# Inverse softmax sums of the first batch by PE transposes, all transposed exponentials copied by ScalarE, and a planner with transfer classes and a clock model

## Chip, core and metric

One core of one Trainium2 chip runs one program. The metric is the device time of one execution in microseconds (us). A kernel's time is the median of its runs.

## What is computed

Attention over 4 batches with 12 heads (448 positions, head size 64), then two feed-forward stages over the 1792 tokens. Everything is float32; the kernel reaches the precision with pairs of fp32r values (high part and rest) and three matmuls for each product.

```python
def _attn_ref(q, k, v, g_q, g_k):
    q_n, k_n = (rmsnorm(q, g_q), rmsnorm(k, g_k))
    scores = scale * np.matmul(q_n, k_n.transpose(0, 1, 3, 2))
    scores = scores - np.max(scores, axis=-1, keepdims=True)
    attn = np.exp(scores)
    attn = attn / (np.sum(attn, axis=-1, keepdims=True) + 1e-09)
    return np.matmul(attn, v)

def _moe_ref(x, w_in, w_out):
    h = x @ w_in
    g = h * np.cos(h)
    return g @ w_out

def _moe2_ref(x, w_in, w_out, a, b):
    h = x @ w_in
    P = a[0] + a[1] * h + a[2] * h2 + a[3] * h3
    Q = 1.0 + np.abs(b[0]) * np.abs(h) + np.abs(b[1]) * h2
    return (P / (Q + 1e-6)) @ w_out
```

## The kernel before, in words

**Stages.** Heads are taken in pairs, six to a batch, so there are 24 pairs `(b, j)`. The six pairs of batch 0 run first. Then, for each batch `b`, the first feed-forward stage (`moe1_first`, `moe1_second`) runs, and between its matmuls stand the pairs of batch `b + 1`. After batch 3 the second stage (`moe2`) runs.

**One pair.** `att_load` loads q and k, `att_norm` normalizes them, `att_t` transposes them on TensorE. `att_s` makes the scores in four chunks; for each chunk VectorE takes the negated row maximum (`mx<-t`) and ScalarE the exponential, whose row sums go to a column of the tile `sums` (`e<-t,mx`). `att_vt` transposes the exponentials on TensorE into PSUM tiles `t` of a ring, and a copy brings them to SBUF as `et`; this copy is a task that either ScalarE or VectorE may take ("AV"). `att_va` multiplies `et` with v into the one PSUM tile `x_ps`, over four blocks `kb`. The last block is followed by a VectorE product with the inverse sums, `rb<-x_ps,rb`. Since `x_ps` has one buffer, the first `x_ps` matmul of the next pair waits for this product.

**Inverse sums.** In `x_ps` the tokens lie along the free dimension, but `sums` has them along partitions. So the function `inverse` (in `att_s`) makes the reciprocals on VectorE and transposes them in 32 x 32 blocks (`rows<-sums`), four transfers write them to DRAM (`rd<-rows`), and two transfers read them back, each row spread over 64 partitions (`rb<-rd`).

**Weights.** Each 768 KB unit of weights `(m, f)` arrives as raw words (`raw<-in_moe_w_in`, `raw<-in_moe_w_out`; `m` 0 and 1 are the first stage's two matrices). `decode` takes it apart: three VectorE steps, a ScalarE copy of the high part, a GpSimd subtraction for the rest. Decoded units are stored to DRAM (`wd`). The first seven are used straight from SBUF (`w`, stored by `wd<-w`); eight more, the list `early`, are decoded into the raw tile, stored by `wd<-raw`, and loaded again by `w<-wd` when one of the seven weight tiles comes free. The first matmuls `h_ps<-g,w` of batch 0 need the units (1,0) to (1,3); (1,0) is one of the seven, (1,1) to (1,3) are `early` ones.

**What sets the order.** The Python code runs through the TensorE order, which is fixed by the code. All work of the other engines is handed to `Clock.do` as tasks with a planned duration and dependencies. `Clock` keeps a model time and emits a task on its engine's in-order queue (V, A, G, or S for the DMA queue of SyncE) when the model says that the engine would take it; `rank` picks among ready tasks. The function `body` rehearses the whole kernel `REHEARSALS` times, derives due times from each rehearsal (`plan`), and builds the program with the due times of the rehearsal with the lowest model time. A task with `size` is a transfer: the model adds `size / RATE` to the time at which the DMA engines are free. So numbers in these calls move instructions, though they are no part of the computation.

All instructions show one line, 277, that of the helper which records them.

Of the kernel before, what the change touches and what calls it, by code (L numbers as in the profile page):

```python
# [11 lines left out]
F32 = mybir.dt.float32  # L12
F32R = mybir.dt.float32r
I32 = mybir.dt.int32
AF = mybir.ActivationFunctionType
# [5 lines left out]
P, NC = 128, 4  # L21
# [7 lines left out]
EPS = 1e-6  # L29
REHEARSALS = 12  # L30
EXP, SIN = "natural_log_exp_and_others", "trig_and_small"
# [9 lines left out]
class Clock:  # L41

    WAIT, LOAD, RATE, QUEUE, LAND, AHEAD = 4.0, 1.28, 0.362, 4.0, 1.25, 1.0
    FROM_PE, TO_PE, LAT = 0.19, 0.11, 0.035
    OVER = {"V": 0.085, "A": 0.1, "G": 0.0, "S": 0.0}

    def __init__(self, due=None):
        self.t, self.n, self.named = 0.0, 0, {}  # L50
        self.free = dict.fromkeys(("V", "A", "G", "S"), 0.0)
        self.todo = {e: [] for e in self.free}
        self.tab, self.dma = None, 0.0
        self.port = {"V": 0.0, "G": 0.0}
        self.slots = deque([0.0] * 8, 8)
        self.due, self.all, self.count = due, [], {}

    def do(
# [44 lines left out]
    def rank(self, k, e, start):  # L103
        other = k.tab is not None and k.tab != self.tab and start - k.ready < self.WAIT
        second = len(k.eng) > 1 and e != next(iter(k.eng))
        if k.due is None:
            return other, k.prio + 2 * second, k.ready, k.n
        return other, k.due + 1.0 * second, k.ready, k.n

# [27 lines left out]
    def step(self, until=math.inf):  # L137
# [25 lines left out]
        if k.size:  # L163
            self.dma = max(self.dma, start + self.LAND) + k.size / self.RATE
            end = max(end, self.dma) + 0.9
            for _ in range(k.parts):
                self.slots.remove(math.inf)
            self.slots.extend([end] * k.parts)
        k.end = end
        k.eng = {eng: k.eng[eng]}  # L170
# [31 lines left out]
    def pe(self, dur):  # L202
        self.t += dur
        while self.step(self.t - self.AHEAD):
            pass

    def plan(self, last):

        due = {}
        for k in reversed(self.all):  # L210
            k.lst = k.need - self.TO_PE
            for x in k.succ:
                k.lst = min(k.lst, x.lst - self.LAT)
            k.lst -= next(iter(k.eng.values())) + (k.size / self.RATE + 2.0 if k.size else 0)
            old = last.get(k.name, math.inf) if last else math.inf
            due[k.name] = k.lst if math.inf in (k.lst, old) else 0.3 * k.lst + 0.7 * old
        return due
# [86 lines left out]
class Kernel:  # L304
# [87 lines left out]
    def decode(self, m, f, keep=True, p=1):  # L392
# [36 lines left out]
        def store():  # L429
# [5 lines left out]
        k = self.raw_load = ck.do(  # L435
            "S", 0.48, load, last, p=p, size=0.786, behind=self.raw_load, name=who + ("load",)
        )
        for i, d in enumerate((0.55, 0.95, 0.95)):
# [11 lines left out]
        k2 = ck.do(  # L450
            "S", 0.39, store, k, p=p, size=0.786, key=("wd", m, f), name=who + ("store",)
        )
# [6 lines left out]
    def load_w(self, m, f):  # L459
# [6 lines left out]

        return t, self.ck.do("S", 0.36, load, ("wd", m, f), p=1, size=0.786)

# [25 lines left out]
    def att_load(self, b, j):  # L494
# [3 lines left out]
        for i, n in ((1, "k"), (0, "q")):  # L498
# [29 lines left out]
            k = ck.do("G", 0.3 if i else 0.35, blank, p=0)  # L528
            s["load"][i] = [k, ck.do("S", 1.95 if i else 2.3, load, p=0 if b == 0 else 1, size=0.23, parts=4 - i)]
        return s  # L530
# [4 lines left out]
    def att_load_v(self, s):  # L535
# [11 lines left out]

        s["vk"] = self.ck.do("S", 1.7, load, p=1, size=0.23, parts=3)

# [107 lines left out]
    def att_s(self, s, c):  # L657
# [43 lines left out]
        def inverse():  # L701
# [4 lines left out]
            nc.vector.reciprocal(t, t)  # L706
            nc.vector.transpose(u, sm)

# [11 lines left out]

        rd = self.rd[s["b"] * NJ + s["j"]]
        k = ck.do("V", 0.66, inverse, *s["ek"], p=1, port=True)
        k = ck.do("S", 1.3, write, k, p=0, size=0.004, parts=4)
        s["smk"][:] = [k]
# [11 lines left out]
    def att_vt(self, s, kb):  # L736
# [26 lines left out]
        n = 2 * S if kb < NM else NC * P  # L763
        et = s["et", kb] = p.tile([P, 2 * S], F32, tag="et", name="et", bufs=2)[:, :n]
        if kb < NM:
            k1 = ck.do("AV", (0.6, 0.69), lambda e: self.copy(e, et[:, : NC * P], tp[0]), p=0)
            k2 = ck.do(
                "AV", (0.5, 0.55), lambda e: self.copy(e, et[:, NC * P :], tp[1][:, : NM * P]), p=0
            )
            tu[0][1].append(k1)  # L770
            tu[1][1].append(k2)
            s["etk", kb] = [k1, k2]
        else:
            k1 = ck.do("AV", (0.6, 0.69), lambda e: self.copy(e, et, tp[0]), p=0)
            tu[0][1].append(k1)
            s["etk", kb] = [k1]

    def att_va(self, s, kb):
# [3 lines left out]
        if kb == 0:  # L782
            ck.need(s["vk"])
            s["xp"] = self.x_ring.tile(ck)
            spread, k = s["rbk"]
            s["rbk"] = ck.do("S", 1.25, spread, k, self.rb_used, p=0, size=0.23, parts=2)
        (xp, users), et, v = s["xp"], s.pop(("et", kb)), s["v"]
# [9 lines left out]
        if kb == NM:  # L797
# [21 lines left out]
            kept.append(k)  # L819
            self.rb_used = k  # L820

    def att_v(self, s, kb):
# [103 lines left out]
    def moe1_second(self, b, d, fs, gs, y):  # L926
# [26 lines left out]
        if fs[-1] == NF - 1:  # L953
# [8 lines left out]

            kept.append(ck.do("S", 0.36, store, k, key=("xd", b, d), size=0.46))

    def load_x(self, b, js=range(NJ), p=1):
        ck = self.ck
        for j in js:
# [7 lines left out]
            self.x[b, j] = x  # L975
            kept.append(ck.do("S", 0.45, load, ("xd", b, j), p=p, key=("x", b, j), size=0.46))

    def moe2(self, tiles, G, after_x):
# [9 lines left out]
        def second(t, fs, gs, wo):  # L988
# [27 lines left out]
            if fs[-1] == NF - 1:  # L1016
                kept.append(ck.do("S", 0.45, lambda: store(o, t), k, size=0.4))

# [346 lines left out]
```

## Time and profile before

| | us |
|---|---|
| median of 3 runs | 1287.27 (1286.4 to 1288.6) |
| the profiled execution | 1285.99 |
| its span, first to last instruction | 1283.8 |
| TensorE busy | 1231.9 (96%) |
| VectorE, ScalarE, GpSimd busy | 899.8, 668.8, 286.9 |
| mean granted TensorE clock | 0.99 of full |

The span is shorter than the execution by 2.2 us, which lie around it. "Busy" is the time in which at least one instruction of the engine ran. TensorE (PE in the rows) is busy almost throughout, so what can be won is its idle time, the stretches at a lower granted clock (PEclk below 1.00), and matmuls that are left out. An idle stretch is put down to the event that ended it. DVE is VectorE, ACT ScalarE, POOL GpSimd, SPq the queue of SyncE, which issues nearly all transfers.

### The profile page before, as it was taken

The numbers are of one execution on the slowest core, as the hardware profiler recorded it, in microseconds if no ns is written. First come the engines' busy times: TensorE is split into PE (matmuls) and PEld (weight loads), VectorE is DVE, ScalarE is ACT, GpSimd is POOL, SyncE is SP. The second block draws the span as 40 slices with busy tenths as digits, with TensorE's granted clock in tenths as the row PEclk, the third lists the DMA queues.
The fourth block names the chain that finished last, engine by engine and source line by source line (L and its number), as shares of the span: only waits on it lengthen the run. The fifth ranks groups of instructions, "written<-read, shape, count | busy, mean of one in ns | idle before, by whom it ended". The sixth has DMA issues, their size and how long they took to land.

```text
span 1283.8 us, 18219 instructions
## 1 busy us (share of the span) xinstructions
PE 1231.9 (96%) x6576; PEld 1051.6 (82%) x6576; DVE 899.8 (70%) x1443; ACT 668.8 (52%) x1277; POOL 286.9 (22%) x363
## 2 busy tenths in 40 slices
PE   6798899899999999999999999999999999999998
PEld 4456667678877778877778999999999999999998
DVE  7787889985778766878766443775767576567663
ACT  6564557653665544755544223675544455554540
POOL 4555355551425231325122110100000000000000
PEclk9899799999999999999999999999999999999999
DMA  4666987877897689888689997624141825132312
GB/s 122 188 189 237 314 313 222 284 259 279 281 330 255 221 305 339 283 288 292 226 311 370 379 372 289 259 74 148 50 148 50 311 109 208 50 148 78 122 48 86
DMA packets 133562, 283.62 MB, mean 221 GB/s; under 512 B 57953, under 2 KB 91745, under 8 KB 133473
## 3 DMA queue, kind: packets, MB, share of 16 engines
q1 hardware_dynamic: 133280, 282.46, 62.7%
q8 instruction: 52, 0.85, 0.3%
q14 instruction: 38, 0.30, 0.1%
q0 software_dynamic: 192, 0.00, 0.0%
HBM read 215.49 MB, written 66.93 MB: 220 GB/s over the span
## 4 chain that ended last, share of the span: by engine, by line
PE 72%; DMA 12%; DVE 6%; ACT 3%; SPq 3%; POOL 2%; issue 2%; POOLq 0%; DVEq 0%; ACTq 0%
PE h_ps L277 43%; PE o_ps L277 18%; PE t L277 8%; DMA rb<-rd 4%; PE x_ps L277 3%; SPq L277 3%; DMA qk<-in_k 2%; DVE w L277 2%; DMA raw<-in_moe_w_out 2%; DMA raw<-in_moe_w_in 2%; DMA w<-wd 2%; DVE k L277 1%; DMA wd<-raw 1%; ACT k L277 1%; POOL w L277 1%
## 5 line engine op out<-in xcount | busy, mean ns | idle before, releaser
L277 PE MATMUL h_ps<-x,w 128*128 128x448 f32 x2250 | 486.4, 369 | 5.0 <-DVE k L277 3.1
L277 PEld LDWEIGHTS h_ps<-x,w 128*128 128x128 f32 x2250 | 418.1, 188 | 50.2 <-issue 10.5
L277 PE MATMUL h_ps<-g,w 128*128 128x448 f32 x1152 | 251.1, 372 | 14.7 <-DMA w<-wd 9.8
L277 PEld LDWEIGHTS h_ps<-g,w 128*128 128x128 f32 x1152 | 214.9, 189 | 42.8 <-issue 9.1
L277 PE MATMUL o_ps<-w,g 128*128 128x384 f32 x1344 | 244.6, 337 | 0.0
L277 PEld LDWEIGHTS o_ps<-w,g 128*128 128x128 f32 x1344 | 237.1, 188 | 1.9
L277 DVE SCALAR_TENSOR_TENSOR w<-raw,w 128x768 int32<-128x768 int32 x128 | 136.1, 1066 | 0.9
L277 ACT ACTIVATE e<-t,mx 128x448 f32<-128x448 f32 x168 | 104.8, 633 | 35.0 <-DVE mx L277 34.8
L277 POOL TENSOR_TENSOR raw<-w,raw 128x768 fp32r<-128x768 f32 x40 | 74.8, 1870 | 195.3 <-ACT raw L277 188.4
L277 PE MATMUL x_ps<-et,v 128*64 128x448 f32 (+1 forms) x384 | 91.6, 568 | 7.5 <-issue 5.9
L277 DVE TENSOR_REDUCE mx<-t 128x1 f32<-128x448 f32 x168 | 95.1, 616 | 5.1 <-PE t L277 4.9
L277 PEld LDWEIGHTS t<-ident,e 128*128 128x128 f32 (+1 forms) x696 | 76.3, 138 | 26.3 <-issue 21.5
L277 PE MATMUL t<-kt,qt 64*128 64x448 f32 (+1 forms) x504 | 85.5, 408 | 9.2 <-DVE kt L277 4.0
L277 PE MATMUL t<-ident,e 128*128 128x128 f32 (+1 forms) x696 | 89.1, 277 | 1.2 <-ACT e L277 1.2
L277 PEld LDWEIGHTS t<-kt,qt 64*128 64x128 f32 (+1 forms) x504 | 51.6, 194 | 41.3 <-issue 18.6
L277 ACT ACTIVATE g<-q 128x448 fp32r<-128x448 f32 x64 | 36.9, 577 | 88.3 <-DVE q L277 88.2
L277 ACT ACTIVATE k<-h_ps,cc 128x448 int32<-128x448 f32 x61 | 38.3, 630 | 64.7 <-PE h_ps L277 64.7
L277 ACT ACTIVATE q<-h_ps,na 128x448 f32<-128x448 f32 x64 | 46.3, 724 | 39.1 <-PE h_ps L277 38.5
L277 ACT ACTIVATE r<-v,cc 128x448 f32<-128x448 f32 x64 | 42.8, 668 | 45.4 <-DVE v L277 44.3
L277 DVE TENSOR_TENSOR q<-q,h_ps 128x448 f32<-128x448 f32 x64 | 39.7, 620 | 37.7 <-ACT w L277 36.5
L277 DVE SCALAR_TENSOR_TENSOR v<-v,r 128x448 f32<-128x448 f32 x64 | 40.0, 625 | 37.1 <-ACT r L277 35.2
L277 DVE TENSOR_TENSOR y<-h_ps,y 128x448 f32<-128x448 f32 x72 | 44.4, 618 | 25.2 <-PE h_ps L277 24.8
(80 smaller groups left out, 1371.4 us busy)
## 6 DMA issues: line engine op xcount, KB each, us to landing
w<-wd SPq DMA_DIRECT2D x168, 768.0 KB
wd<-raw SPq DMA_DIRECT2D x40, 768.0 KB
raw<-in_moe_w_in SPq DMA_DIRECT2D x32, 768.0 KB
raw<-in_moe_w_out SPq DMA_DIRECT2D x32, 768.0 KB
wd<-w SPq DMA_DIRECT2D x24, 768.0 KB
xd<-x SPq DMA_DIRECT2D x24, 448.0 KB
x<-xd SPq DMA_DIRECT2D x24, 448.0 KB
rb<-rd SPq DMA_DIRECT2D x48, 112.0 KB
```

The source lines that it names most:

```text
L277: inst = fn(*args, **kw)
```

## The change

1. **Inverse sums in batch 0.** `inverse` leaves out its block transpose, and no `rd` and `rb` transfers are made. A new function `att_rows`, called before the last `x_ps` block, makes eight PE transposes of a column of `sums` that is broadcast to 128 columns, into two PSUM tiles, and ScalarE copies two 64 x 448 pieces to `rb`. Batches 1 to 3 keep the way through DRAM.
2. **Copies of `et`.** All go to ScalarE.
3. **Planner.** 40 rehearsals in place of 12. A transfer's `size` is now its own time in us, negative for writes, with latencies READ 2.2 and WRITE 1.5 and a delay LATE 1.0 until it counts as done. TensorE's model time passes more slowly after idle stretches. A change of ScalarE's table no longer ranks behind everything; it adds 2.0 to the due time.

The diff, cut to its core:

```diff
-REHEARSALS = 12
+REHEARSALS = 40
...
     def rank(self, k, e, start):
-        other = k.tab is not None and k.tab != self.tab and start - k.ready < self.WAIT
+        other = k.tab is not None and k.tab != self.tab
...
-        return other, k.due + 1.0 * second, k.ready, k.n
+        return k.due + 1.0 * second + 2.0 * other, k.ready, k.n
...
         if k.size:
-            self.dma = max(self.dma, start + self.LAND) + k.size / self.RATE
-            end = max(end, self.dma) + 0.9
+            lag = self.READ if k.size > 0 else self.WRITE
+            self.dma = max(self.dma, end - k.eng["S"] / k.parts + lag) + abs(k.size)
+            end = max(end, self.dma)
...
-            "S", 0.48, load, last, p=p, size=0.786, behind=self.raw_load, name=who + ("load",)
+            "S", 0.48, load, last, p=p, size=2.9 if m % 2 == 0 else 2.5, behind=self.raw_load, name=who + ("load",)
...
-            "S", 0.39, store, k, p=p, size=0.786, key=("wd", m, f), name=who + ("store",)
+            "S", 0.39, store, k, p=p, size=-1.9, key=("wd", m, f), name=who + ("store",)
...
-        return t, self.ck.do("S", 0.36, load, ("wd", m, f), p=1, size=0.786)
+        return t, self.ck.do("S", 0.36, load, ("wd", m, f), p=1, size=2.0)
...
-            nc.vector.transpose(u, sm)
+            if s["b"]:
+                nc.vector.transpose(u, sm)
...
-        k = ck.do("V", 0.66, inverse, *s["ek"], p=1, port=True)
-        k = ck.do("S", 1.3, write, k, p=0, size=0.004, parts=4)
+        k = ck.do("V", 0.66 if s["b"] else 0.45, inverse, *s["ek"], p=1, port=True)
+        if s["b"] == 0:
+            s["rbk"] = None, k
+            return
+        k = ck.do("S", 1.3, write, k, p=0, size=-0.3, parts=4)
...
-            k1 = ck.do("AV", (0.6, 0.69), lambda e: self.copy(e, et[:, : NC * P], tp[0]), p=0)
...
+        for t, to, x, dur in parts:
+            eng, dur = "A", dur[0]
+            k = ck.do(eng, dur, lambda e="A", to=to, x=x: self.copy(e, to, x), p=0)
...
+        if kb == NM and s["b"] == 0:
+            self.att_rows(s)
...
+    def att_rows(self, s):
+
+        nc, ck = self.nc, self.ck
+        ck.need(s["rbk"][1])
+        tiles = [self.at_tile() for _ in range(2)]
+        for h, (tp, _) in enumerate(tiles):
+            for k in range(h * NM, h * NM + NC):
+                a = (k - h * NM) * P
+                nc.tensor.transpose(
+                    tp[:, a : a + P], s["sm"][:, k : k + 1].to_broadcast([P, P]), self.ident[:]
+                )
+        ck.pe(0.77)
+
+        def rows():
+            rb = s["rb"] = self.at_p.tile([P, S], F32, tag="rb", name="rb", bufs=1)
+            for h, ((tp, _), r) in enumerate(zip(tiles, HALVES)):
+                nc.scalar.activation(rb[r], tp[r, h * SL : h * SL + S], AF.Copy)
+
+        s["rbk"] = ck.do("A", 1.0, rows, self.rb_used, p=0)
```

What it moves is seen at two places. On TensorE, pair 0 of batch 0, before (`x_ps<-et,v` are the blocks of the product with v, `t<-kt,qt` the scores of the next pair, `t<-ident,e` the transposed exponentials):

```order
L277 MATMUL x_ps<-et,v 64x448 x2
L277 MATMUL t<-kt,qt 128x448 x6
L277 MATMUL x_ps<-et,v 64x448 x2
L277 MATMUL t<-kt,qt 128x448 x6
L277 MATMUL t<-ident,e 128x128 x7
```

And now:

```order
L293 MATMUL x_ps<-et,v 64x448 x2
L293 MATMUL t<-kt,qt 128x448 x6
L293 MATMUL t<-ident,sums_63 128x128 x8
L293 MATMUL x_ps<-et,v 64x448 x2
L293 MATMUL t<-kt,qt 128x448 x6
L293 MATMUL t<-ident,e 128x128 x7
```

The eight transposes are the only difference; six such blocks stand in the program, one for each pair of batch 0, and the rest of TensorE's order is as it was.

On SyncE's queue, from the end of batch 0's attention on, before (stores of decoded units, `wd<-raw`, and loads of them, `w<-wd`):

```order
L277 DMA rb<-rd 64x448 x2
L277 DMA raw<-in_moe_w_out 128x1536
L277 DMA wd<-w 128x1536
L277 DMA raw<-in_moe_w_out 128x1536
L277 DMA wd<-w 128x1536
L277 DMA wd<-raw 128x1536 x2
L277 DMA w<-wd 128x1536
L277 DMA raw<-in_moe_w_in 128x6x256
L277 DMA wd<-raw 128x1536
L277 DMA w<-wd 128x1536
L277 DMA raw<-in_moe_w_in 128x6x256
L277 DMA w<-wd 128x1536
```

And now:

```order
L293 DMA raw<-in_moe_w_out 128x1536
L293 DMA wd<-w 128x1536
L293 DMA wd<-raw 128x1536
L293 DMA raw<-in_moe_w_in 128x6x256
L293 DMA wd<-raw 128x1536 x2
L293 DMA raw<-in_moe_w_in 128x6x256 x2
L293 DMA wd<-raw 128x1536
L293 DMA w<-wd 128x1536 x2
L293 DMA raw<-in_moe_w_out 128x1536
L293 DMA wd<-raw 128x1536
L293 DMA w<-wd 128x1536 x2
```

Four stores of `early` units now stand before the first load of one, in place of two, and the first two loads follow each other directly. On GpSimd's queue the steps of these four units stand ahead of the small transfer `ab<-in_moe_a`, which in the order before stood ahead of all of them. In the whole program 85 copies `et<-t` leave VectorE for ScalarE; the number of table loads on ScalarE is 21 in both.

## Rows read from the trace of the kernel before

**Rows 1.** The page: span, TensorE's share, and the group of transposes of exponentials.
```profile
span 1283.8 us, 18219 instructions
...
PE 1231.9 (96%) x6576; PEld 1051.6 (82%) x6576; DVE 899.8 (70%) x1443; ACT 668.8 (52%) x1277; POOL 286.9 (22%) x363
...
L277 PE MATMUL t<-ident,e 128*128 128x128 f32 (+1 forms) x696 | 89.1, 277 | 1.2 <-ACT e L277 1.2
```

**Rows 2.** Busy us of each engine by stretch, granted clock, DMA share, GB/s.
```profile
0.00:102.00 102.00, 81.63 (x462) 48.92 (x462) 78.53 (x153) 62.24 (x156) 55.63 (x103) 0.95 0.60 169
56.00:62.00 6.00, 6.00 (x27) 3.65 (x27) 3.79 (x8) 2.31 (x5) 3.90 (x6) 0.69 0.52 176
78.00:88.00 10.00, 8.95 (x41) 4.98 (x42) 8.68 (x16) 6.21 (x17) 7.20 (x9) 0.83 0.64 205
102.00:142.00 40.00, 28.75 (x131) 24.15 (x130) 33.33 (x45) 20.61 (x33) 15.45 (x11) 0.83 0.74 269
132.00:137.00 5.00, 2.30 (x6) 1.33 (x5) 4.97 (x6) 1.99 (x3) 1.81 (x1) 0.50 1.06 375
137.00:142.00 5.00, 5.00 (x20) 3.84 (x20) 4.96 (x8) 3.17 (x5) 2.16 (x2) 0.53 0.63 221
240.00:255.00 15.00, 10.78 (x58) 8.04 (x58) 15.00 (x21) 9.99 (x22) 7.96 (x11) 1.00 0.86 282
```

**Rows 3.** Waits of PE over the whole span: us, times, longest.
```profile
PE h_ps L277 <- DMA w<-wd: 11.7, 5, 5.0
PE t L277 <- DVE qk L277: 9.6, 2, 9.2
PE x_ps L277 <- issue: 5.9, 1, 5.9
```

**Rows 4.** Timeline, 38 to 64 us: start, duration, instruction, idle time before it.
```profile
38.88 1.09 PE L277 MATMUL t<-ident,qk 128*128 128x128 f32 x8
...
39.81 0.93 PE L277 MATMUL t<-ident,e 128*128 128x128 f32 x7
...
55.09 0.62 DVE L277 TENSOR_TENSOR rb<-x_ps,rb 128x448 f32<-128x448 f32 x1 [4.86 <-DMA rb<-rd]
...
55.82 1.76 PE L277 MATMUL x_ps<-et,v 128*64 128x448 f32 x4 [5.87 <-issue]
...
57.51 1.97 PE L277 MATMUL t<-ident,qk 128*128 128x128 f32 x8
```

**Rows 5.** Timeline, 96 to 142 us: the first loads of early units and what they wait for.
```profile
110.67 1.38 PE L277 MATMUL h_ps<-x,w 128*128 128x448 f32 x6
...
112.62 0.20 ACT L277 ACTIVATE bb<-ab 128x2 f32<-128x2 f32 x1 [7.36 <-DMA ab<-in_moe_b]
...
115.53 4.29 SPq L277 DMA_DIRECT2D wd<-raw  x2
...
119.92 0.37 SPq L277 DMA_DIRECT2D w<-wd  x1
...
125.80 0.85 PE L277 MATMUL h_ps<-g,w 128*128 128x448 f32 x3 [2.04 <-DMA w<-wd]
...
131.69 1.46 PE L277 MATMUL h_ps<-g,w 128*128 128x448 f32 x3 [5.04 <-DMA w<-wd]
...
135.85 1.46 PE L277 MATMUL h_ps<-g,w 128*128 128x448 f32 x3 [2.70 <-DMA w<-wd]
```

**Rows 6.** Groups of copies of `et`, 0 to 102 us: busy us, mean ns of one.
```profile
L277 DVE COPY et<-t 128x512 f32<-128x512 f32 x12 | 8.2, 681 | 0.0
L277 DVE COPY et<-t 128x384 f32<-128x384 f32 x10 | 5.5, 550 | 1.2 <-issue 1.1
L277 ACT ACTIVATE et<-t 128x512 f32<-128x512 f32 x12 | 7.1, 594 | 2.4 <-issue 1.9 <-PE t L277 0.5
L277 ACT ACTIVATE et<-t 128x384 f32<-128x384 f32 x8 | 3.9, 491 | 0.1
```

**Rows 7.** Waits of VectorE over the whole span, the product with the inverse sums.
```profile
DVE rb L277 <- DMA rb<-rd: 33.0, 15, 5.5
```

More of the change, by code (lines that the diff above doesn't have):

```diff
@@ L41 @@
 class Clock:
[L45 removed]
+    WAIT, LOAD, QUEUE, AHEAD, LATE = 4.0, 1.28, 4.0, 1.0, 1.0
+    READ, WRITE, WINDOW = 2.2, 1.5, 3.413
     FROM_PE, TO_PE, LAT = 0.19, 0.11, 0.035
@@ L56, in __init__ @@
         self.due, self.all, self.count = due, [], {}
+        self.window, self.half = [0, 0.0], True
     def do(
@@ L103, in rank @@
     def rank(self, k, e, start):
-        other = k.tab is not None and k.tab != self.tab and start - k.ready < self.WAIT
+        other = k.tab is not None and k.tab != self.tab
         second = len(k.eng) > 1 and e != next(iter(k.eng))
         if k.due is None:
-            return other, k.prio + 2 * second, k.ready, k.n
-        return other, k.due + 1.0 * second, k.ready, k.n
+            return other and start - k.ready < self.WAIT, k.prio + 2 * second, k.ready, k.n
+        return k.due + 1.0 * second + 2.0 * other, k.ready, k.n
     def candidate(self, e):
@@ L168, in step @@
             self.slots.extend([end] * k.parts)
+            end += self.LATE
         k.end = end
@@ L202, in pe @@
     def pe(self, dur):
-        self.t += dur
+        while dur > 1e-9:
+            n = int(self.t // self.WINDOW)
+            if n > self.window[0]:
+                idle, part = n > self.window[0] + 1, self.window[1] / self.WINDOW
+                self.half = idle or part < (0.62 if self.half else 0.5)
+                self.window = [n, 0.0]
+            rate = 0.53 if self.half else 1.0
+            d = min(dur / rate, (n + 1) * self.WINDOW - self.t + 1e-6)
+            self.window[1] += d
+            self.t += d
+            dur -= d * rate
         while self.step(self.t - self.AHEAD):
@@ L213, in plan @@
                 k.lst = min(k.lst, x.lst - self.LAT)
-            k.lst -= next(iter(k.eng.values())) + (k.size / self.RATE + 2.0 if k.size else 0)
+            k.lst -= next(iter(k.eng.values())) + (abs(k.size) + self.READ + self.LATE if k.size else 0)
             old = last.get(k.name, math.inf) if last else math.inf
@@ L528, in att_load @@
             k = ck.do("G", 0.3 if i else 0.35, blank, p=0)
-            s["load"][i] = [k, ck.do("S", 1.95 if i else 2.3, load, p=0 if b == 0 else 1, size=0.23, parts=4 - i)]
+            s["load"][i] = [k, ck.do("S", 1.95 if i else 2.3, load, p=0 if b == 0 else 1, size=1.3 if i == 0 else 0.9, parts=4 - i)]
         return s
@@ L546, in load @@
                 nc.sync.dma_start(out=v[r, 2 * NM], in_=src[h, SM:])
-        s["vk"] = self.ck.do("S", 1.7, load, p=1, size=0.23, parts=3)
+        s["vk"] = self.ck.do("S", 1.7, load, p=1, size=1.1, parts=3)
     def att_norm(self, s):
@@ L764, in att_vt @@
         et = s["et", kb] = p.tile([P, 2 * S], F32, tag="et", name="et", bufs=2)[:, :n]
+        parts = [(tu[0], et[:, : NC * P], tp[0], (0.6, 0.69))]
         if kb < NM:
-            k1 = ck.do("AV", (0.6, 0.69), lambda e: self.copy(e, et[:, : NC * P], tp[0]), p=0)
[L767 to L776, printed above, removed]
+            parts.append((tu[1], et[:, NC * P :], tp[1][:, : NM * P], (0.5, 0.55)))
+        s["etk", kb] = []
+        for t, to, x, dur in parts:
+            eng, dur = "A", dur[0]
+            k = ck.do(eng, dur, lambda e="A", to=to, x=x: self.copy(e, to, x), p=0)
+            t[1].append(k)
+            s["etk", kb].append(k)
     def att_va(self, s, kb):
@@ L785, in att_va @@
             spread, k = s["rbk"]
-            s["rbk"] = ck.do("S", 1.25, spread, k, self.rb_used, p=0, size=0.23, parts=2)
+            if spread:
+                s["rbk"] = ck.do("S", 1.25, spread, k, self.rb_used, p=0, size=0.7, parts=2)
+        if kb == NM and s["b"] == 0:
+            self.att_rows(s)
         (xp, users), et, v = s["xp"], s.pop(("et", kb)), s["v"]
@@ L820, in att_va @@
             self.rb_used = k
+    def att_rows(self, s):
[14 more added lines that the diff above has]
+        s["rbk"] = ck.do("A", 1.0, rows, self.rb_used, p=0)
+        for _, users in tiles:
+            users.append(s["rbk"])
     def att_v(self, s, kb):
@@ L961, in store @@
                 )
-            kept.append(ck.do("S", 0.36, store, k, key=("xd", b, d), size=0.46))
+            kept.append(ck.do("S", 0.36, store, k, key=("xd", b, d), size=-1.1))
     def load_x(self, b, js=range(NJ), p=1):
@@ L975, in load_x @@
             self.x[b, j] = x
-            kept.append(ck.do("S", 0.45, load, ("xd", b, j), p=p, key=("x", b, j), size=0.46))
+            kept.append(ck.do("S", 0.45, load, ("xd", b, j), p=p, key=("x", b, j), size=1.15))
     def moe2(self, tiles, G, after_x):
@@ L1016, in second @@
             if fs[-1] == NF - 1:
-                kept.append(ck.do("S", 0.45, lambda: store(o, t), k, size=0.4))
+                kept.append(ck.do("S", 0.45, lambda: store(o, t), k, size=-0.95))
         def before(fs, gs, order):
```

## The prediction

> **What bounds the kernel now.** I read the page first. TensorE is busy for 1231.9 of 1283.8 us [rows 1], so the work on TensorE sets the end and the other engines count where TensorE waits for them or runs at half clock. The second view, the waits of TensorE, shows how little there is to win [rows 3]: 9.6 us for normalized q and k, nearly all of it the first load, which this change leaves alone; 11.7 us in five pieces for weights loaded back (`w<-wd`); and 5.9 us before a single `x_ps` matmul. The third view, busy time by stretch [rows 2], says where it lies: TensorE is idle for 20.4 of the first 102 us (102.00 - 81.63), the attention of batch 0, and for 11.3 of the next 40 (40.00 - 28.75), the first matmuls of the feed-forward stage. What follows can give back a few us only. The fourth view, the timeline, says what holds each of the two large waits.
>
> The wait of 5.87 us before `x_ps` has no releaser named. VectorE's product with `rb` ended 0.1 us before it (55.09 + 0.62 against 55.82), and had itself stood idle for 4.86 us for the transfer `rb<-rd` [rows 4]. So the way of the sums through DRAM was late, the one `x_ps` buffer stayed taken, and TensorE stood still. After it the clock is down: 0.69 granted in 56 to 62 us [rows 2], and eight transposes are spread over more time (1.97 us) than before it (1.09) [rows 4]. Since the clock has two levels, 2.4 and 1.2 GHz, 0.69 over 6 us means 3.7 us at the lower one ((1 - 0.69) x 2 x 6).
>
> The second large wait is three pieces of 2.04, 5.04 and 2.70 us, each ended by a `w<-wd` load [rows 5]. The first of these loads was issued at 119.92, right behind two stores of decoded units that held SyncE's queue for 4.29 us; and the matmul it feeds started at 125.80, 5.9 us after the issue. The stores were late since the decode was late: ScalarE stood 7.36 us for the small transfer `ab` and could only then go on with the decoded units [rows 5].
>
> **The change, part by part.** The sum is made against the profiled execution, 1286.0 us (span 1283.8 and 2.2 around it); the median shown is 1.3 us above it.
>
> *A, batch 0's sums.* Gone: the stall, 5.87 us, and the half-rate work behind it, 1.9 us (half of 3.7, TensorE being busy for all of 56 to 62). No other pair stalled this way [rows 3]. Gone too are 36 transfers from SyncE's queue and six block transposes from VectorE; they are worth nothing by themselves, because neither queue nor engine holds TensorE elsewhere in this stage. Added: 48 transposes on TensorE. The nearest row are eight transposes whose successor starts 0.93 us later (38.88 to 39.81) [rows 4], so six blocks take 5.6 us. That they cost nothing is excluded, since TensorE takes them in order and is the bound; at half clock a block took up to 1.97 us, so the other end is 11.8 us. I take 5.6, because most of this stage runs at full clock (0.95 over 0 to 102) [rows 2].
>
> Here a rule of the Trainium skill speaks against the change. "TensorE: Matmul & The Clock Gate", Part 4, PE-mode transpose, gives about 275 ns for a transpose and says that the full clock does not engage for them; by it 48 would be 13.2 us (an estimate from that page). The trace agrees on the duration of one, 277 ns mean [rows 1], but not on what a row of them costs, since they overlap.
>
> The two ScalarE copies to `rb` for each pair lie between a 384- and a 512-element copy, 0.49 to 0.59 us each [rows 6]; they run beside the last `x_ps` block and the 26 matmuls of other pairs that follow before `x_ps` is wanted again. Nothing on the path. Their cover is gone if ScalarE's queue is late; that is a rival below. The new wait on TensorE, for the reciprocals, is short work on VectorE of sums that were complete before the first block of the pair; everything on TensorE would queue behind it.
>
> In 78 to 88 us TensorE is idle for 1.05 us and at half clock for 3.4 us ((1 - 0.83) x 2 x 10) [rows 2], behind exponentials and a copy that were late. VectorE is busy 8.68 of these 10 us and loses copies, while ScalarE gains them. Idle time and half-rate work together are 1.05 + 1.7 = 2.75 us; I take half, 1.4. A is 5.87 + 1.9 + 1.4 - 5.6 = 3.6 us.
>
> *B, early weights.* Now four stores stand before the first load of an early unit instead of two, and their decode stands before `ab` on GpSimd. VectorE has room for it: it gives up 13.7 us of copies in the first 102 us (8.2 + 5.5) [rows 6]. The first two loads can then be issued when weight tiles come free, after the six matmuls that end at 112.05, while the matmul that waited first was due at 123.8 (125.80 - 2.04) [rows 5]: 11.7 us, and a load took 5.9. The third stands behind one more store, of a unit decoded after `ab`; it is what is late next, and I leave 2.5 us for it. So of 9.8 us of waiting (2.04 + 5.04 + 2.70) 7.3 go. The clock was at 0.50 and 0.53 in 132 to 142, where TensorE was busy for 2.30 and 5.00 us [rows 2]; all of the first and 94% of the second were at the lower level, and half of that, 3.5 us, goes with the wait. B is 10.8 us. Its ends are nothing, if the wait only moves to another unit, and 13.3.
>
> *C, later batches.* 63 more copies leave VectorE. In 240 to 255 us VectorE is busy for all 15.00 us, while TensorE is busy for 10.78 [rows 2]: 4.2 us lost to VectorE. I take half, 2.1. All other tasks of batches 1 to 3 are reordered too; these stretches lose little now, and I take nothing, with 4 us either way for the range. Table loads stay at 21.
>
> Sum: 3.6 + 10.8 + 2.1 = 16.5 us. 1286.0 - 16.5 = 1269.5, and with 1.3 for the median 1270.8; I say 1271.
>
> **The rivals.** *ScalarE becomes the bound in batch 0.* It was busy for 62.2 of 102 us [rows 2]. Now it takes 22 copies (12 x 0.594 + 10 x 0.491 = 12.0 us), and twelve `rb` copies (5.9 to 7.1), so some 81 us, with steps of four decodes on top, in a stage that is to shrink to 98. For: exponentials, q, k and the copies now queue on one engine. Against: its copies follow each other closely, and the copies on it are shorter than on VectorE (594 against 681 ns). If it binds, A turns into a loss of some 3 us: 1271 + 3.6 + 3 = 1278. The Trainium skill, "TensorEngine Tiling (Array Packing)", PSUM Bottleneck, advises using both engines for emptying PSUM, which is this rival. No row here yet shows ScalarE full.
>
> *The early loads stay late*, since reordered stores or raw loads hold SyncE's queue for them: B is lost but for 2 us, 1271 + 8.8 = 1280.
>
> *Transposes that don't overlap.* A row of eight that does not overlap takes 2.2 us (8 x 277 ns [rows 1]) in place of 0.93; six rows are 7.7 us more, 1279. The overlap in the rows speaks against it.
>
> *Slower: the sums' transfers of batches 1 to 3.* 18 pairs still fetch `rb` through DRAM, and the new order may put it behind more 768 KB loads. VectorE already waits 33.0 us for `rb` in 15 cases, of which only one stopped TensorE [rows 3, 7]. Each that does would cost what the one did, 5.87 + 1.9 = 7.8 us. Two would cost most of the gain; from the third on it is slower: 1271 + 23.4 = 1294. Against it: the matmuls between give most of these pairs cover now.
>
> *The planner's order changes nothing on the chip* where it was meant to: only the stall goes and the transposes come, 5.87 + 1.9 - 5.6 = 2.2 us, 1285 in the median.
>
> **How the numbers follow.** The forecast, 1260 to 1276, has 0.62: its low end takes all that B and C could give and 4 us more (1271 - 2.5 - 2.1 - 4 = 1262, rounded out), its high end 4 us less and a part of the transposes' upper end. ScalarE 0.1, late loads 0.1, transposes 0.04, no effect 0.05, slower 0.09. The range 1260 to 1281 holds the forecast and the three rivals that end by 1280; it leaves out the last two (0.14), and little below. A difference under 0.2% (2.6 us) can't be told from no change. Faster takes the forecast and the first three rivals, 0.86; same 0.05; slower 0.09.
>
> **What would show it.** Right: no `x_ps` wait of several us in the first 100 us and a clock at full in 50 to 62; the last `x_ps` of batch 0 some 4 us earlier; no more than one wait for `w<-wd` before 140 us, of under 3 us. Six rows of eight transposes with a successor after 0.93 us. VectorE's busy time lower by 50 us or more, ScalarE's higher by about as much. Wrong: TensorE waiting for `et` or `e` of ScalarE for more than 5 us in batch 0; early loads issued later than the stage's first matmuls; or a `rb<-rd` that ends an `x_ps` wait in a later batch.

## Result and the profile after

| us | before | after |
|---|---|---|
| median of 4 runs, measured together | 1287.43 (1286.40 to 1288.60) | 1276.57 (1273.58 to 1278.12) |
| profiled execution | 1285.99 | 1273.58 |

The ratio is 0.9913 [0.9893, 0.9933]: 10.9 us faster, where 16.5 were forecast. The profiled execution is the fastest of its four, so its gain of 12.4 us is a little above the median's.

The page after, with the same group as in [rows 1]:

```profile
span 1271.8 us, 18275 instructions
...
PE 1232.2 (97%) x6624; PEld 1055.3 (83%) x6624; DVE 860.4 (68%) x1360; ACT 710.0 (56%) x1373; POOL 273.6 (22%) x356
...
L293 PE MATMUL t<-ident,e 128*128 128x128 f32 (+1 forms) x696 | 88.6, 277 | 0.0
```

VectorE is busy 39 us less (50 were expected) and ScalarE 41 us more: the copies have moved. TensorE's busy time stays, with 48 transposes more. The stretches of [rows 2], after:

```profile
0.00:102.00 102.00, 83.97 (x491) 52.81 (x492) 79.12 (x136) 78.14 (x190) 59.77 (x100) 0.98 0.65 192
...
56.00:62.00 6.00, 6.00 (x41) 3.69 (x39) 5.66 (x9) 5.59 (x13) 3.19 (x5) 1.00 0.84 289
78.00:88.00 10.00, 9.85 (x64) 5.71 (x63) 8.16 (x15) 7.24 (x18) 3.99 (x10) 1.00 0.56 193
102.00:142.00 40.00, 34.45 (x174) 28.26 (x173) 29.65 (x43) 23.58 (x43) 17.47 (x22) 0.96 0.88 317
234.00:249.00 15.00, 10.82 (x58) 8.03 (x57) 14.45 (x23) 10.24 (x20) 8.66 (x10) 1.00 0.78 254
```

The clock in 56 to 62 is 1.00 (0.69 before), and TensorE works 5.7 us more in 102 to 142. The last row is 6 us earlier than its counterpart, since the same work stands 6 to 7 us earlier there; TensorE's share of it hasn't changed (10.78 before). ScalarE is busy 78 of the first 102 us, near the 81 of the prediction. The waits of TensorE, as [rows 3]:

```profile
PE t L293 <- DVE qk L293: 9.6, 2, 9.3
PE h_ps L293 <- DVE k L293: 9.5, 7, 3.2
PE t L293 <- ACT e L293: 4.3, 4, 2.6
PE h_ps L293 <- DVE qt L293: 3.8, 1, 3.8
PE t L293 <- POOL qk L293: 2.6, 2, 2.3
PE h_ps L293 <- DMA w<-wd: 2.2, 4, 0.8
```

The `x_ps` stall is gone and loads hold TensorE for 2.2 us instead of 11.7. `h_ps` now waits 9.5 us for VectorE's `k` (5.7 before, in pieces of at most 1.6 us); new are its wait for `qt` and one for `qk` of GpSimd. Where the time went shows when the same matmuls of the same order start in both profiled executions (the last column is before minus after, from unrounded times):

| matmul | before | after | after is ahead by |
|---|---|---|---|
| first transposes of q, k of pair 1 | 16.8 | 19.1 | -2.3 |
| `x_ps` behind the second block of sums | 45.6 | 49.4 | -3.9 |
| transposes of e after the old stall | 59.3 | 56.1 | 3.2 |
| `x_ps` behind the third block | 64.7 | 62.4 | 2.3 |
| `x_ps` after the first `h_ps` | 72.3 | 76.0 | -3.6 |
| batch 0's last `x_ps` (end) | 102.1 | 105.4 | -3.3 |
| transposes of q, k in the first `h_ps` stretch | 122.1 | 128.7 | -6.6 |
| scores behind the early loads | 137.2 | 132.1 | 5.1 |
| first transposed e of batch 1 | 160.4 | 156.8 | 3.6 |
| last `x_ps` of batch 3 (end) | 668.2 | 657.3 | 10.9 |

Three losses stand in this table beside the gains. The timeline of TensorE after shows them, and one block of transposes (start, duration, instruction, idle time before it):

```profile
19.10 1.12 PE L293 MATMUL t<-ident,qk 128*128 128x128 f32 x4 [2.27 <-POOL qk L293]
...
35.13 1.09 PE L293 MATMUL t<-ident,sums 128*128 128x128 f32 x8
36.15 0.97 PE L293 MATMUL x_ps<-et,v 64*64 64x448 f32 x4
...
73.03 1.49 PE L293 MATMUL h_ps<-x,w 128*128 128x448 f32 x3 [3.81 <-DVE qt L293]
74.32 1.70 PE L293 MATMUL t<-ident,e 128*128 128x128 f32 x7
...
123.42 4.86 PE L293 MATMUL h_ps<-x,w 128*128 128x448 f32 x15 [3.24 <-DVE k L293]
```

**At 17 us** TensorE waits for normalized q and k of pair 1. In the new order pair 1's second sum of squares stands behind two scaled copies on VectorE and runs at 13.71 instead of 11.99, and GpSimd's chain for q and k begins at 14.90 instead of 13.34. The first decode of a weight unit stands among VectorE's next steps; it begins at 14.66 and so can't have delayed the start of that chain. Within the chain another 0.7 us are lost.

**At 69 us** the first `h_ps` of the feed-forward stage waits 3.81 us for `qt`, which is no operand of it. Up to here the tiles of `t` come from a ring of seven, five `at_ps` and two `early_ps`; then the two `early_ps` places become `h_ps`. Counted in the program, 71 tiles are taken before this point, and after the change 77, two more for each of three pairs. So the ring stands elsewhere, and the two places now are those of pair 5's transposed q and k (the last pair of batch 0, counted from 0), which were only just made. The matmul can't write before ScalarE and VectorE have read them, and ScalarE comes to them late (timeline of ScalarE after):

```profile
69.78 0.58 ACT L293 ACTIVATE x<-rb 128x448 fp32r<-128x448 f32 x1
70.25 0.85 ACT L293 ACTIVATE w<-w 128x768 fp32r<-128x768 f32 x1
70.98 0.63 ACT L293 ACTIVATE sq<-qk 128x512 f32<-128x512 f32 x1
71.50 0.69 ACT L293 ACTIVATE qt<-t,gg 128x512 fp32r<-128x512 f32 x1
...
118.36 0.20 ACT L293 ACTIVATE bb<-ab 128x2 f32<-128x2 f32 x1 [7.89 <-DMA ab<-in_moe_b]
118.59 0.64 ACT L293 ACTIVATE k<-h_ps,cc 128x448 int32<-128x448 f32 x1
```

**At 120 us** the last two of these rows show why `h_ps` waits for `k`: in ScalarE's queue, ahead of `k<-h_ps`, stands a step on the coefficients `ab`, and that tiny transfer is late. VectorE's queue is held by the same coefficients (`na<-ab`, the first row below, from VectorE's timeline). The issue stands on GpSimd's queue behind decode steps, more of them than before:

```profile
116.08 0.17 DVE L293 TENSOR_SCALAR na<-ab 128x4 f32<-128x4 f32 x1 [3.28 <-DMA ab<-in_moe_a]
...
110.55 1.84 POOL L293 TENSOR_TENSOR raw<-w,raw 128x768 fp32r<-128x768 f32 x1 [2.30 <-ACT raw L293]
112.33 0.62 POOL L293 DMA_DIRECT2D ab<-in_moe_a  x1
112.95 0.54 POOL L293 DMA_DIRECT2D ab<-in_moe_b  x1
```

The gain of this stretch is in the loads: the first two are issued at 114.74 (119.92 before), behind the stores and 14.8 us ahead of the first `h_ps<-g,w` at 129.51:

```profile
114.74 0.93 SPq L293 DMA_DIRECT2D w<-wd  x2
```

### The profile page after: what moved, and what is told of

Same layout as the page of the kernel before. It is cut to its first block, busy times and chain, and to the rows that moved or that the text cites. A ratio compares the mean times of both kernels' runs of the same rounds, so it can differ in the third digit from the quotient of the medians.

```text
span 1271.8 us, 18275 instructions
## 1 busy us (share of the span) xinstructions
PE 1232.2 (97%) x6624; PEld 1055.3 (83%) x6624; DVE 860.4 (68%) x1360; ACT 710.0 (56%) x1373; POOL 273.6 (22%) x356
## 4 chain that ended last, share of the span: by engine, by line
PE 80%; DMA 4%; DVE 2%; ACT 1%; issue 1%; POOL 1%; SPq 0%; DVEq 0%; POOLq 0%; ACTq 0%
PE h_ps L293 48%; PE o_ps L293 18%; PE t L293 9%; PE x_ps L293 4%; DMA w<-wd 3%; DMA raw<-in_moe_w_in 1%; DVE w L293 1%; DVE k L293 0%; DMA rb<-rd 0%; ACT k L293 0%; POOL w L293 0%; ACT w L293 0%; DVE x L293 0%; ACT L293 0%; SPq L293 0%
## 5 line engine op out<-in xcount | busy, mean ns | idle before, releaser
L293 PE MATMUL h_ps<-g,w 128*128 128x448 f32 x1152 | 248.2, 369 | 8.1 <-DVE k L293 6.2
L293 DVE SCALAR_TENSOR_TENSOR w<-raw,w 128x768 int32<-128x768 int32 x128 | 139.7, 1095 | 1.1
L293 ACT ACTIVATE et<-t 128x512 f32<-128x512 f32 (+1 forms) x168 | 82.2, 554 | 25.4 <-PE t L293 25.1
L293 DVE SCALAR_TENSOR_TENSOR k<-k,h_ps 128x448 f32<-128x448 int32 x61 | 37.7, 619 | 57.2 <-ACT k L293 56.9
L293 ACT ACTIVATE r<-v,cc 128x448 f32<-128x448 f32 x64 | 42.8, 669 | 48.7 <-DVE v L293 47.6
L293 ACT ACTIVATE raw<-w 128x768 fp32r<-128x768 f32 x40 | 33.8, 847 | 58.0 <-DVE w L293 50.8
```

Of the source, the lines that this page charges most:

```text
L293: inst = fn(*args, **kw)
```

## The experiments

Every run is compared with the kernel before, measured beside it: 1285.58 us beside e1 to e4, 1284.83 beside e5 to e8 and 1286.80 beside e9 to e12. Between these groups the ratios say more than the microseconds. "Batch 0" is the end of its last `x_ps`, "stage" the time from there to batch 1's first transposed e, "batches 1 to 3" from there to the last `x_ps`, each in the profiled execution alone. The same kernel differs there by up to 2 us (the change and e5), and e1's profiled execution is the slowest of its ten, 3.8 us above the median.

| run | us | ratio [95%] | batch 0 | stage | batches 1 to 3 |
|---|---|---|---|---|---|
| before | | 1 | 102.1 | 58.3 | 507.8 |
| the change, first measured | 1276.57 | 0.9913 [0.9893, 0.9933] | 105.4 | 51.4 | 500.5 |
| e1 rows only | 1285.97 | 1.0010 [0.9998, 1.0022] | 101.8 | 50.8 | 512.1 |
| e2 copies only | 1290.89 | 1.0057 [1.0037, 1.0077] | 105.1 | 51.1 | 512.9 |
| e3 planner only | 1283.12 | 0.9978 [0.9963, 0.9993] | 100.4 | 62.8 | 501.4 |
| e10 rows and copies | 1298.08 | 1.0093 [1.0069, 1.0117] | 113.4 | 56.8 | 503.4 |
| e11 all but copies | 1279.15 | 0.9943 [0.9921, 0.9965] | 102.3 | 52.9 | 504.5 |
| e12 all but rows | 1281.66 | 0.9963 [0.9951, 0.9974] | 104.1 | 60.6 | 502.2 |
| e5 the whole change again | 1276.49 | 0.9930 [0.9905, 0.9955] | 105.2 | 52.4 | 502.5 |
| e4 and ring turned | 1283.27 | 0.9980 [0.9967, 0.9994] | 99.7 | 59.9 | 505.3 |
| e6 and `ab` early | 1271.01 | 0.9885 [0.9848, 0.9922] | 104.4 | 47.6 | 502.6 |
| e7 ring and `ab` | 1273.48 | 0.9905 [0.9874, 0.9935] | 99.8 | 52.0 | 505.4 |
| e8 ring, `ab`, start | 1274.68 | 0.9914 [0.9883, 0.9944] | 102.3 | 49.8 | 505.5 |
| e9 transposes twice | 1277.07 | 0.9930 [0.9906, 0.9954] | 108.2 | 50.0 | 503.9 |

### One part alone

**e1**, the kernel before with the sums of batch 0 by transposes:

```diff
...
+        if s["b"] == 0:
+            s["rbk"] = None, k
+            return
...
+        if kb == NM and s["b"] == 0:
+            self.att_rows(s)
...
```

> The kernel before with the inverse sums of batch 0 by PE transposes, and nothing else of the change. Theory A (the sums give little by themselves: a stall of 5.9 us and 1.9 us of half-rate work go, 48 transposes cost 5.6 us, and six more PSUM tiles shift the ring so that the first h_ps matmul of batch 0 waits for q and k copies): 1284 to 1289 us, no x_ps wait of several us before 100 us, and a new wait of h_ps of 1 to 4 us between 65 and 80 us. Rival (the sums are what the change gains by): 1279 us or less.

The stall is gone and batch 0 is 0.3 us shorter, not 3.6: a wait of `h_ps` for `kt`, 3.59 us at 69.46, has come in, the ring's shift again, under the old planner. The early loads went forward too (three stores stand ahead of the first load instead of two; 0.5 us of `w<-wd` waits before 160), a thing this edit doesn't touch: with other tasks the planner makes another order everywhere. At 258 us the kernel was 11.7 us ahead; it lost this in batches 1 to 3 and behind them, 4.6 of it in one wait for `k` at 677.

**e2**, the kernel before with all copies of `et` on ScalarE:

```diff
...
-            k1 = ck.do("AV", (0.6, 0.69), lambda e: self.copy(e, et, tp[0]), p=0)
+            k1 = ck.do("A", 0.6, lambda e="A": self.copy(e, et, tp[0]), p=0)
```

> The kernel before with all copies of et on ScalarE, and nothing else of the change. Theory D (VectorE, freed of the copies, decodes early units sooner, so their stores come before the first load): waits for w<-wd before 145 us fall from 9.8 to under 4 us, the time is 1277 to 1283, while the x_ps wait for rb stays. Rival M (the new transfer model in the planner puts the stores ahead): waits for w<-wd stay at 7 us or more and the time is within 3 us of 1287.

The waits for early loads go here as well, yet the kernel is slower: `x_ps` waits 3.2 us at 57 and 1.9 at 87, and `t` 5.4 us in seven pieces for `kt`. The view puts the first of these down to ScalarE's `sq`, which is no operand; VectorE's product with `rb` ended 0.1 us before it (56.78 + 0.61 against 57.49), behind other steps of VectorE. The second is the product again, which waited 1.36 us for `rb<-rd`.

**e3**, the change without its rows and its copies, so the planner alone:

```diff
...
-        for t, to, x, dur in parts:
-            eng, dur = "A", dur[0]
-            k = ck.do(eng, dur, lambda e="A", to=to, x=x: self.copy(e, to, x), p=0)
+        for t, to, x, dur in parts:
+            k = ck.do("AV", dur, lambda e, to=to, x=x: self.copy(e, to, x), p=0)
...
-        if kb == NM and s["b"] == 0:
-            self.att_rows(s)
```

> The changed kernel with the sums through DRAM in all batches and the copies of et free to go to ScalarE or VectorE, so the planner's part alone. Rival M: waits for w<-wd before 145 us under 4 us, time 1277 to 1282. Theory D: these waits stay at 6 us or more, and the time is 1284 to 1290.

No load holds TensorE for long before 145 us, but one `h_ps` waits 6.9 us for `k` at 122, and two `x_ps` stalls stand in batch 0 (2.06 and 2.35). Both stalls end with VectorE's product, which was held by VectorE's other steps; the transfer `rb<-rd` kept it for 0.25 us at most. The time lies between the two expectations; the later batches have the gain of the whole change (501.4).

So three edits that alone give +0.4, +5.3 and -2.5 us against the medians beside them give -8 to -11 together. No sum over edits can be made here.

### Two parts

**e10** is e1 and e2 together; **e11** the change with `et` copies free for both engines; **e12** the change with the block transposes and DRAM transfers of batch 0 kept.

```diff
 e11
-            k = ck.do(eng, dur, lambda e="A", to=to, x=x: self.copy(e, to, x), p=0)
+            k = ck.do("AV", dur, lambda e, to=to, x=x: self.copy(e, to, x), p=0)
 e12
...
-        if s["b"] == 0:
-            s["rbk"] = None, k
-            return
...
-        if kb == NM and s["b"] == 0:
-            self.att_rows(s)
```

> The kernel before with batch 0's sums by PE transposes and all copies of et on ScalarE, under the planner of before. Theory (the gain in batches 1 to 3 is the planner's): from the first transposed exponential of batch 1 to the last x_ps 508 to 514 us as in the other programs of that planner (508, 512, 513), not 500 to 505, and the whole 1284 to 1292. Rival (rows and copies together make the gain): that stretch 500 to 505 and the whole 1275 to 1280.

> The changed kernel with the copies of et free for ScalarE or VectorE again. Theory (copies are worth little in batches 1 to 3, and crowd ScalarE in batch 0): batch 0 ends at 100 to 104 us in place of 105.3, batches 1 to 3 take 500 to 506 us, the whole 1272 to 1280. Rival (VectorE's relief is what shortens batches 1 to 3): that stretch takes 507 us or more, the whole 1281 or more.

> The changed kernel with batch 0's inverse sums through DRAM as before. Theory (stall and transposes nearly balance): the last x_ps of batch 0 ends at 101 to 107 us, with x_ps waits for rb of 2 to 8 us in all in place of the 48 transposes, and the whole at 1273 to 1281. Rival (the transposes are the main gain): batch 0 ends at 108 us or later and the whole at 1283 or more.

e10 is above what either theory gave, although its batches 1 to 3 are short under the old planner, as its rival had it; batch 0 took 113.4 us, with waits for GpSimd's `qk` (1.9) and for `kt` (2.5 and 3.6). In e11 the `w<-wd` waits are back, 7.2 us in two pieces, with one store ahead of the first load; e11 stays within its theory's range. In e12 `x_ps` stalls again (1.73 and 1.88 at 41 and 67 us) and `h_ps` waits 5.4 us; its time lies between the two expectations. As in e3, both stalls end with VectorE's product, which followed other steps of VectorE without a gap and so didn't wait for a transfer: under the new planner the way through DRAM was in time, and VectorE was late. By the ratios the copies are worth some 1.7 us within the whole (0.9943 against 0.9930) and the rows some 4.2 (0.9963), but the intervals of e11 and e12 touch that of e5, so only the order is likely.

### The three losses, one by one

**e4** turns the ring, so that `h_ps` takes the two places after those of q and k; otherwise it is the change.

```diff
-        turn, at_n = iter_tiles([at_ps] * 5 + [early_ps] * 2), [0]
+        turn, at_n = iter_tiles([early_ps] * 2 + [at_ps] * 5), [0]
```

> The changed kernel with the two PSUM tiles that later become h_ps taken from the first two places of the ring of seven in place of the last two. Theory (the 3.8 us wait of h_ps at 73 us is for the copies of q and k of the next pair, whose PSUM tiles lie where h_ps is put): that wait falls under 0.7 us, no half clock between 70 and 80 us, 4 to 5 us less: 1271 to 1273 us. Rival (ScalarE is late with q and k in any case, and what is not lost there is lost at the scores that follow): the wait goes but the last x_ps of batch 0 comes no earlier than now, at 105 us less 1, and the time stays within 2 us of 1276.6.

**e5** is the change unchanged, to have it on the same chip as the following three.

> The changed kernel once more, unchanged, beside the next three on one chip. Expected 1274 to 1278 us, and in its profile the waits of its first profile: h_ps at 73 us for q and k of about 3.8 us, h_ps near 123 us for VectorE of about 3 us.

**e6** issues the two `ab` transfers near 24 us, before batch 0's work on GpSimd fills up. The order of every other instruction on every engine is that of the change.

```diff
-        nc.gpsimd.dma_start(out=ab[:, 0:4], in_=a["moe2_a"].partition_broadcast(P))
-        nc.gpsimd.dma_start(out=ab[:, 4:6], in_=a["moe2_b"].partition_broadcast(P))
+        ab = self.ab
...
         take(cur, 8)
+        ab = self.ab = const_p.tile([P, 6], F32, name="ab")
+        nc.gpsimd.dma_start(out=ab[:, 0:4], in_=self.a["moe2_a"].partition_broadcast(P))
+        nc.gpsimd.dma_start(out=ab[:, 4:6], in_=self.a["moe2_b"].partition_broadcast(P))
```

> The changed kernel with the two small transfers ab issued early, in a gap of GpSimd near 24 us, in place of behind the fourth early decode; the order of the four other engines is the same row by row. Theory (ScalarE's wait for ab holds the first activations, and so the h_ps matmul near 123 us): ScalarE's wait of 7.9 us and the wait of h_ps fall away, under 1 us left, the first early units are loaded as before, 2 to 4 us less than the changed kernel beside it. Rival (VectorE's weight decode holds the activations anyway): the wait for ab goes, but h_ps still waits over 2 us and the time stays within 1 us.

**e7** has both edits.

> The ring's places turned as in e4 and ab issued early. Theory (what e4 won in batch 0, 5.7 us at its last x_ps, was given back at the wait for ab): the h_ps wait of 5.8 us near 120 us falls under 1.5 us and the time is 5 to 9 us below e4's, at 1274 to 1278. Rival (the stretch from 100 to 145 us is held by the decode of early units, VectorE or the loads): the wait moves to the second matmuls or to scores, and the time stays within 2 us of e4's.

e5 repeats the change: 1276.49 us, with `h_ps` waiting 3.8 us for `qt` and 4.3 for `k`.

e4's wait at 69 is gone, its batch 0 ends 5.7 us before that of the change, and the kernel is 6.7 us slower (0.9980 against 0.9913 and 0.9930). Neither theory had that. Up to that wait every queue has the order of the change, so the ring is its cause; 1.4 of the 5.7 us were ahead of it (pair 5's transposes start at 66.19 and 67.61) and are small waits whose cause stays open. e4's timeline (GpSimd, ScalarE, TensorE) shows where it went:

```profile
107.61 0.54 POOL L293 DMA_DIRECT2D ab<-in_moe_b  x1
...
115.32 0.20 ACT L293 ACTIVATE bb<-ab 128x2 f32<-128x2 f32 x1 [10.20 <-DMA ab<-in_moe_b]
...
120.28 6.17 PE L293 MATMUL h_ps<-x,w 128*128 128x448 f32 x18 [5.81 <-DVE k L293]
...
139.43 1.49 PE L293 MATMUL t<-kt,qt 64*128 64x448 f32 x5 [4.12 <-ACT e L293]
```

The `ab` transfer was issued 5.3 us earlier than in the change, but ScalarE resumed only 3.0 us earlier; TensorE, ahead by 5.7, waits 5.81 instead of 3.24, which takes 2.6 us of this, and has more of the work behind it at the half clock (the 18 matmuls take 6.0 us to their successor instead of 5.3), which takes 0.7. At 126 us 2.4 are left. What makes it slower comes later: a wait of 4.12 us for an exponential of ScalarE (1.15 in the change) with half clock behind it (0.53 granted in 142 to 146), after which it is 2.8 us behind at batch 1's first transposed e, and longer batches 1 to 3. From 70 us on the planner has given the queues beside TensorE another order, so this is no price of the ring alone.

e6 shows that the wait for `ab` is real on its own: 5.5 us against e5, above the 2 to 4 expected; every run of e6 (1269.9 to 1271.9) is below every run of e5 (1275.1 to 1276.9). Its timeline of TensorE and its stretch 102 to 142:

```profile
127.68 0.85 PE L293 MATMUL h_ps<-g,w 128*128 128x448 f32 x3 [2.16 <-DMA w<-wd]
```

```profile
102.00:142.00 40.00, 36.45 (x196) 30.36 (x193) 34.73 (x53) 27.02 (x52) 16.80 (x21) 1.00 0.93 332
```

The wait for `k` at 120 is gone, the clock is full, and a load is what is late next (2.16 us). With `ab` early the ring's edit costs 2.5 us instead of 6.7 (e7 against e6), though batch 0 is still 4.6 us shorter; e7 is 9.8 us below e4, where 5 to 9 were expected, and its wait for `k` is gone. So batch 0's end no longer sets the time by itself: in e6 and e7 an early load is late next (2.16 and 2.46 us), and the rest of the order differs too.

**e8** is e7 with the first decode tied behind pair 1's normalization, and pair 0's scaled copies behind pair 1's sum of squares:

```diff
...
+        tie = self.sq_used if s["b"] == s["j"] == 0 else None
...
+        self.w32_used[0] = st[1]["kn"][-1]
```

> e7 with VectorE's first steps in the order of the kernel before: the first weight decode waits for pair 1's normalized q and k, and the scaled copies of pair 0 stand behind pair 1's sum of squares. Theory: the wait of TensorE near 17 to 19 us for q and k of pair 1 (2.3 us) falls under 0.7 us, batch 0 ends 2 to 3 us sooner than in e7, and the time falls by as much. Rival: what is won is lost before 145 us, time within 1.5 us of e7's.

The wait at 17 goes (16.77 instead of 18.91 for pair 1's transposes), but smaller waits for `et` and `qk` have taken it back by 33 us, batch 0 ends 2.5 us later, and the whole is 1.2 us slower: the rival.

**e9** issues each of the six blocks of transposes twice; the rows of all other engines are the same.

```diff
-            for k in range(h * NM, h * NM + NC):
+            for k in [*range(h * NM, h * NM + NC)] * 2:
```

> The changed kernel with each of the 48 transposes of batch 0's inverse sums issued twice; all other rows of all engines as in the changed kernel. Theory (TensorE is the bound in batch 0, so a block costs its 0.93 us): 4.5 to 6.5 us more than the changed kernel's 1276.5, so 1281 to 1283, and the last x_ps of batch 0 ends 4 to 6 us later than at 105.3. Rival (ScalarE is the bound there and TensorE has slack): under 2.5 us more, 1276 to 1279.

A doubled block in the timeline of TensorE:

```profile
35.05 1.96 PE L293 MATMUL t<-ident,sums 128*128 128x128 f32 x16
36.95 0.97 PE L293 MATMUL x_ps<-et,v 64*64 64x448 f32 x4
```

Sixteen take 1.90 us to the successor, 0.95 for eight. By the starts of the same matmuls in e5 and e9, each doubled block moves its successor by 0.8 to 0.9 us, 5.1 in all, but batch 0 got only 3.0 us longer, which is in neither expectation. The rest was taken up by waits that stood there already: 1.4 us behind the first two blocks, around which ScalarE was busy for 7.95 of 8 us (38 to 46, e5), and 0.7 at the `h_ps` wait at 69. Then the `h_ps` wait at 120 fell from 4.30 (e5) to 1.83, and the ratio is that of e5 (0.9930). As long as `ab` is late, these transposes add nothing that the runs can tell.

## Why the prediction was right or wrong

Direction and range were right, the size was not: 1276.6 against 1271, just past the forecast's own upper edge of 1276. That it lies in the stated range is in part luck. Up to the last `x_ps` of batch 3 the profiled executions give -3.3 us for A, 6.9 for the stage of B and 7.3 for batches 1 to 3, where 3.6, 10.8 and 2.1 were forecast: two terms fell short by 10.8 us together, and the third, for another reason than the one given, made up for 5.2 of it.

**A, batch 0: the step that failed.** Forecast +3.6, measured -3.3 (table of starts). Its first terms hold: stall and half-rate work were put at 7.8 us, and after gains 7.1 between the second block and 56 us. The time of a block holds: 0.93 forecast, 0.95 by e9, 1.02 in the row above, where the next instruction is of another size; that each is paid in full doesn't, since e9's batch 0 paid 3.0 of 5.1 us. In 78 to 88 us TensorE idles 0.15 us and runs at full clock, better than the half that was taken. What failed is the list of what the change adds. I counted transposes as time on TensorE and not as two PSUM tiles for each pair. Three pairs take six, the ring of seven stands elsewhere, and `h_ps` falls on tiles in use: 3.81 us, and 5.9 with the half clock behind it (2.3 to -3.6 in the table). e1 shows the same wait under the old planner, e4 shows it go with the ring. The second loss, 2.3 us at 17, comes from the order of VectorE's first steps: 1.6 us of it is the later sum of squares, ahead of any decode; e8 put that and the decode back together, so the share of the decode stays open. The prediction didn't compare the start of the queues.

The Trainium skill, "TensorE: Matmul & The Clock Gate", Part 4, was rightly not followed here: its 275 ns is the duration of one transpose (277 in the page), but a row of sixteen passes in 1.90 us, and the clock that it says would not engage was granted at 1.00 in 56 to 62, a stretch that includes such a block between other matmuls.

**B, early loads: right, then partly taken back.** 10.8 forecast; over the first `h_ps` stretch after gains 11.7 (-6.6 to 5.1), and no load holds TensorE for over 0.8 us. But 3.3 us went ahead of that (-3.3 to -6.6), in the wait for `ab` and the half clock behind it, and 1.5 after it (5.1 to 3.6), with waits of 1.17 us for `k` and 1.15 for an exponential: 6.9 in all. The prediction had quoted `ab`, as the reason why the decode was late, and had even said that four units now stood ahead of it on GpSimd; it didn't price that for ScalarE, where the matmuls' own `k` stands behind it, nor for VectorE. e6 gives the price: 5.5 us. The reason given, more room on VectorE, is not the cause by itself: the loads also went forward in e1, which takes only block transposes from it, and in e3, which takes no copies. e2, with the copies alone, and e11, where loads are late again without them, fit it. Which part of the change moved the loads stays open.

**C, 2.1 us: wrong as told.** The stretch that was to gain has TensorE busy for 10.82 us of 15 (10.78 before) with VectorE still at 14.45, and a wait of 2.6 us for ScalarE's exponential stands there now:

```profile
245.11 0.88 PE L293 MATMUL t<-kt,qt 64*128 64x448 f32 x5 [2.60 <-ACT e L293]
```

Batches 1 to 3 instead gave 7.3 us over their whole length (507.8 to 500.5; 5.3 by e5's 502.5), for which the prediction had 2.1 and 4 either way. All kernels with the new planner have 500.5 to 505.5 there, e3 with neither rows nor copies among them (501.4). Of those with the old one e1 and e2 have 512 to 513, but e10, with rows and copies, has 503.4. So the new planner is enough for the short stretch, but it isn't shown to be the cause: e10 got one without it. Which of the planner's rules matters was not tried.

**The rivals.** ScalarE bound in batch 0 had 1278, near the result, but not by its mechanism: the waits for `et` and `e` there are 0.7 us, and e9's 1.4 us behind the first two blocks say that ScalarE held TensorE for somewhat more than these show. A full queue took part, since `qt` stood behind three other tasks; e4, with ScalarE busy for 80.3 us of 102, has no such wait. Late loads, transposes without overlap, and `rb` transfers in later batches didn't come about: no `x_ps` waits for anything over 0.2 us after.

## What to carry to other kernels

When an edit takes more tiles from a rotating buffer, count on from there: who gets which place at the next hand-over is part of its cost. A tiny transfer whose result stands in an in-order queue ahead of main work should be issued long before; it was worth 5.5 us of 1276, half of what the whole change gave, and that version (e6, 1271.0) is the fastest of all here. Where a planner orders everything, test with edits that leave all other rows alike (e6, e9), since each part alone (e1 to e3) changes all queues and its time says little about the part.

## What the runs showed of the hardware

The transfer of `ab`, under 4 KB, reached ScalarE 4.1 us after its issue before the change (108.53, GpSimd's timeline, to 112.62, [rows 5]), 5.4 us after it (112.95 to 118.36) and 7.7 us in e4 (107.61 to 115.32), with the DMA engines busy for 0.74 to 0.88 of 102 to 142 us. Issued at 24 us in e6, it landed after 3.9 us. The Trainium skill, "DMA: Bandwidth & Descriptors", Anatomy of one DMA, gives about 2.0 us as the fixed part; these rows have two to four times that.

Small steps on GpSimd are not of fixed length. The same product of 128 x 16 elements, in the chain for pair 1's q and k, before and after:

```profile
13.62 0.21 POOL L277 TENSOR_TENSOR t<-r 128x16 f32<-128x16 f32 x1
```

```profile
15.36 0.93 POOL L293 TENSOR_TENSOR t<-r 128x16 f32<-128x16 f32 x1
```

After, VectorE ran a step of the weight decode in the same 0.96 us (15.26 to 16.22). That the one slows the other is a guess from this pair of rows and was not measured by itself.

The granted clock in the views says nothing about the first 25 us. The same fifteen matmuls with the same order before them, after and in e9, with the stretch around them:

```profile
20.87 4.07 PE L293 MATMUL t<-kt,qt 128*128 128x448 f32 x15
...
19.00:25.00 6.00, 5.90 (x24) 4.09 (x25) 4.94 (x11) 5.08 (x15) 4.58 (x9) 1.00 0.38 134
```

```profile
20.81 3.28 PE L293 MATMUL t<-kt,qt 128*128 128x448 f32 x15
...
19.00:25.00 6.00, 5.96 (x31) 4.24 (x31) 4.95 (x11) 5.01 (x15) 4.58 (x8) 1.00 0.39 137
```

They run at different rates (4.0 and 3.2 us to their successors), while the clock reads 1.00 in both. The first record of the clock in the two traces stands at 25.1 and 22.6 us, and the views take it as full before that.
